# A gated linear attention and MLP kernel: the PSUM bank or shared buffer of every tile named in a table

## The chip, the core and the metric

The kernel runs on one core of one Trainium2 chip, as one program: TensorE multiplies matrices into PSUM, VectorE (DVE), ScalarE (ACT) and GpSimd (POOL) do elementwise work, SyncE (SP) issues nearly all DMAs. Each engine takes its instructions in the order written, and semaphores order the engines against each other. The metric is the device time of one execution in microseconds.

## The reference

Gated linear attention with a recurrent state, then a feed-forward block with a layer norm ahead of it and a residual around it. Shapes: 4 batches, 8 heads, 768 steps, 48 columns a head, so rows of 384; the hidden width is 1536. q, k, v, alpha and g_ln are float32; w_ch1 and w_ch2 come as float64.

```python
for t in range(S):
    state = alpha[:, :, t, :, None] * state + einsum('bhd,bhe->bhde', k[:, :, t], v[:, :, t])
    y[:, :, t] = einsum('bhd,bhde->bhe', q[:, :, t], state)
x = y.transpose(0, 2, 1, 3).reshape(B, S, H * D)
xn = (x - mean(x)) / sqrt(var(x) + 1e-06) * g_ln
out = x + maximum(xn @ w_ch1, 0.0) @ w_ch2
```

## The kernel before

The 768 steps are cut into 6 chunks of 128. The unit of attention is one chunk of one batch, 24 in all, written as generators (`attention`, turns a to x in the order below). For a unit, ScalarE takes the log of alpha (L343), TensorE sums it along the chunk with a triangular matrix (L348, L355) and ScalarE exponentiates the sum (L358, L359); DVE scales q and k by it (L363, L365). q and k are turned round, by TensorE (L422) for the first 12 units and by DVE and DMAs (L404, L150, L416) after that. TensorE makes scores (L435, L450), DVE copies them under a mask out of PSUM into `at` (L464), TensorE makes the state's update (L479) and the output (L515). The state is gated on DVE and POOL (L492, L494). ScalarE reads the output (L524, L525), stores it away in DRAM (L539) and normalises it (L547 to L557), and the row is turned round into `xT` (L573, or L563 and L150).

The feed-forward block of chunk 0 is a plain matrix product: `hidden` (L598, relu in L601) and `project` (L610, L614). For chunks 1 to 5 both products use a scheme of fewer block products with sums ahead of and behind them: DVE adds blocks of xT, of w1, of the hidden values and of w2 (`combine_x` L870, `combine_first` L845, `combine_hidden` L704, `combine_weights` L675); `hidden_product` (L901) and `product` (L722) multiply the blocks, and what they leave in PSUM is copied by ScalarE (L913, L746) or added by DVE and POOL (L917 to L930, L736 to L742). The weights come as float64 and are rounded to float32 in eight pieces by DVE and ScalarE (L247 to L261) in the first 100 us.

The order of all this is written out by hand. `ORDER` (L28) is a string in which each letter advances one generator by one step, and `tc.manual_schedule()` keeps that order on every engine. Waits are worked out by the tile framework from the tiles that an instruction reads and writes.

Tiles come from pools. A tag has `bufs` buffers, and the tiles of a tag share them: `bank` is six PSUM banks, `row` eight buffers of 384 columns, `sum` twelve buffers of 512 columns (the turned q and k, the sums of blocks and the copies `u`), `in` six input buffers, `gate` four, `few` five, `mid` three. Which of its buffers a tile gets is the framework's choice. The first instruction that writes a tile waits until all that used the tile before it in the same buffer has ended, whatever that other tile held. PSUM has two more banks, `updates`, that no tag shares.

In the code before, `combine_hidden` makes its six or seven sum tiles together at its first step (L688), `combine_x` its five (L856), `product` and `hidden_product` their three `u` tiles at the first product of a group (L716, L888), and `attention` its gate tile where the row of gates is sent off (L375).

Of the kernel before, what the change touches and what calls it, by code (L numbers as in the profile page):

```python
# [50 lines left out]

WHERE = {
}


def pick(marks, usual=0):
# [4 lines left out]
def kernel(  # L61
# [36 lines left out]
    nc = tc.nc  # L98
# [11 lines left out]
    assert out.shape == (B, S, DM) and B * P <= 512 and DM + 2 * NP <= 512  # L110

    cpool = ctx.enter_context(tc.tile_pool(name="const", bufs=1))
    raw = ctx.enter_context(tc.tile_pool(name="raw", bufs=B // 2))
    stage = ctx.enter_context(tc.tile_pool(name="stage", bufs=STAGED))
    work = ctx.enter_context(tc.tile_pool(name="work", bufs=2))
    dram = ctx.enter_context(
        tc.tile_pool(name="dram", bufs=B, space=bass.MemoryType.DRAM))
    ps = ctx.enter_context(tc.tile_pool(name="ps", bufs=2, space=bass.MemoryType.PSUM))

    nc.scalar.preload_act_table_set("natural_log_exp_and_others")  # L120

# [205 lines left out]
    def attention(c, b):  # L327
# [44 lines left out]
        ends = slice(P - 1, P) if whole else slice(HS - 1, P, HS)  # L372
        ne = 1 if whole else 2
        row = dram.tile([2, 2 * 64 * NP], FP32, name="row", tag="row")
        gate = work.tile([P, 2, NP], FP32, name="gate", tag="gate", bufs=B)  # L375
        nc.sync.dma_start(row[:ne], eq_of(c, b)[ends].rearrange("o p i c -> o (p i c)"))
        yield
        def load_next():
# [84 lines left out]
        else:  # L463
# [2 lines left out]
                data=scores.pop((c, b)).rearrange("k p s t -> k (p s) t"),  # L466
                mask=mask_of_halves.unsqueeze(1).broadcast_to([P, 2 * NP, HS]))
        yield
        with nc.allow_non_contiguous_dma(reason="two rows to columns"):
            nc.sync.dma_start(gate[:, :ne], row[:ne].rearrange("o (p r) -> r o p", p=NP))  # L470
        yield
# [182 lines left out]
    def summer(name, op):  # L654
        return getattr((nc.vector, nc.gpsimd)[pick(sides[name])], op)
# [57 lines left out]

    def product(c, n):
        if n == SECOND[0]:
            u = [work.tile([P, 512], FP32, name="u", tag="sum", bufs=12) for i in range(3)]  # L716
            win["u"] = [u[i // 2][:, i % 2 * HM:][:, :HM] for i in range(5)]
        acc = held.pop(("S", c, FOLLOWS[n])) if n in FOLLOWS else ps.tile(
            [P, HM], FP32, name="ops", tag="bank", bufs=6)
        lhs, rhs = blocks_of(c)[1][n], weights_ready()[n]  # L720
        for j in range(NT):
            nc.tensor.matmul(acc, lhs[:, j], rhs[:, j], start=j == 0 and n not in FOLLOWS,  # L722
                             stop=j == NT - 1 and n not in FOLLOWS.values(),
                             skip_group_check=True)
        if n in FOLLOWS.values():
            held["S", c, n] = acc
        yield
        e, f, g, q4, r8 = win["u"]
# [15 lines left out]
        copied = {0: e, 2: f, 9: f, 14: g, 13: q4, 8: r8}  # L744
        if n in copied:
            copy(out=copied[n], in_=acc)  # L746
        if n in (15, 3):
            add(o(0))
        elif n == 11:
            sub(o(0))  # L750
        elif n == 18:
            sub(o(1))
            sub(o(3))
        elif n == 10:
            add(o(2))
        elif n == 1:
            sub(o(7))
        elif n in (4, 17):
            add(o(4))
        elif n == 6:  # L760
            sub(o(1))
        elif n == 2:
            late(o(1), e)
            late(o(1), f, "sub")
            send(c, 0)
        elif n == 5:
            nc.vector.tensor_sub(g, acc, g)
        elif n == 19:
            sub(o(3))
            send(c, 1)  # L770
        elif n == 9:
            late(f, g, "sub")
            late(o(2), f, "sub")
            late(o(3), f, "sub")
        elif n == 12:
            sub(o(5))
            add(o(7))
        elif n == 13:
            late(o(5), q4)
            late(o(5), g, "sub")  # L780
            late(r8, q4, "sub")
            late(o(7), r8)
            late(o(6), r8)
            if c + 1 == NCB:
                send(c, 2, slice(0, HM))
                send(c, 3, slice(HM, DM))
        elif n == 7:
            add(o(5))
            if c + 1 == NCB:
                send(c, 2, slice(HM, DM))  # L790
            else:
                send(c, 2)
                send(c, 3, slice(HM, DM))
        elif n == 16:
            add(o(6))
            send(c, 3, slice(0, HM))
        yield
# [51 lines left out]

    def combine_x(c):  # L850
        b = x_blocks(c)
        new = []
        if c + 1 == NCB:
            buffers_of_last()
            new = late_of["x"]
        for i in range(0 if new else 5):  # L856
            t = work.tile([P, NT, P], FP32, name=f"sum{i}", tag="sum", bufs=12)
            t = t.rearrange("p a t -> p (a t)")
            new += [t[:, k * HB * P:(k + 1) * HB * P] for k in range(2)]
        t101, t103, t100, m7, t102, m10, m9, m13, m8 = new[:9]  # L860
        add, sub = "tensor_add", "tensor_sub"
        ready = x_ready(c)
        for n, op, out, x, y in (
                (None, sub, t101, b[1], b[3]), (2, sub, t100, b[4], b[5]),
                (1, add, t103, b[2], t100), (7, add, m7, t101, t103),
                (14, sub, t102, b[0], t100), (10, sub, m10, t102, t101),
                (3, sub, t101, t101, b[5]), (9, sub, m9, b[4], b[0]),
                (5, add, b[4], b[2], b[4]), (13, sub, m13, b[3], t103),
                (8, sub, m8, b[1], t102)):
            summer("X", op)(out, x, y)  # L870
            if n is not None:
                ready[n] = out
            yield
# [8 lines left out]
    def hidden_product(c, r, n):  # L882
# [2 lines left out]
            if c + 1 < NCB:  # L885
                hT_of[c] = work.tile([P, NJ, B, P], FP32, name="hT", tag="hT", bufs=1)
        if n == FIRST[0]:
            for i in range(3):  # L888
                u = late_of["u"][i] if c + 1 == NCB else work.tile(
                    [P, 512], FP32, name="u", tag="sum", bufs=12)  # L890
                first_of["u", c, i] = u.rearrange("p (j t) -> p j t", j=2)
# [11 lines left out]
        if n in JOINS.values():  # L903
            held["F", c, n] = acc
        yield
        u0, u1, u2 = (first_of["u", c, i] for i in range(3))
# [4 lines left out]
        copied = {3: c5, 7: c4, 5: c2, 1: u0, 10: u1, 9: u2, 8: u2, 11: c1, 2: c0}  # L911
        if n in copied:
            nc.scalar.copy(out=copied[n], in_=acc)  # L913
        if n == 5:
            add_late(c2, c2, u1)
        elif n == 6:
            add(c4, acc, c4)  # L917
            add_late(c4, c4, u2)
        elif n == 4:
            sub(c2, c2, acc)  # L920
        elif n == 14:
            add(c0, acc, c0)  # L922
        elif n == 1:
            add_late(c0, c0, u0)
        elif n == 13:
            add(c1, acc, c1)
            add_late(c1, c1, u2)
            add_late(c5, c5, u2)
        elif n == 12:
            sub(c5, c5, acc)  # L930
        elif n == 0:
            nc.scalar.activation(out=c3, in_=acc, func=AFT.Relu)
# [70 lines left out]
```

## Time and profile before

| | |
|---|---|
| Median of 3 runs | 422.12 us (419.4 to 424.57) |
| Profiled execution | 420.36 us |
| Its span, from the first to the last instruction | 418.6 us |
| Granted TensorE clock | 1.000 |
| DMA traffic | 61.25 MB, mean 146 GB/s |

In the profile, PE is TensorE's matmuls, PEld its weight loads (they overlap), SPq SyncE's queue of DMA issues. A line such as L464 is the line of the kernel that issued an instruction, with out<-in by the names of the tiles. A float32 matmul leaves about two records. In a timeline row come the start and the length in us, then engine, line, operation, tiles and shapes; xN merges N like instructions in a row, and a bracket gives the idle time of the engine before it and what ended that. In a list of waits come the total, the number and the longest; in a list of groups busy time and the mean in ns; in a table of windows the length of the stretch and then the busy time of PE, PEld, DVE, ACT and POOL, each with a count, the granted clock, the DMA share and GB/s.

### The profile page before, as it was taken

Reading aid. Unit: us, or ns where it says so; the run is one execution under the profiler, and the core shown is the slowest. Engines: PE = TensorE matmul, PEld = TensorE weight load, DVE = VectorE, ACT = ScalarE, POOL = GpSimd, SP = SyncE. Lnnn points to the kernel's source line nnn. Section 1 sums busy time; section 2 is a strip of 40 time slices with the busy share of each in tenths; the row PEclk is TensorE's granted clock in tenths of the full one; section 3 lists DMA queues with packets and bytes.
Section 4 is the critical chain, followed back from the end, with each engine's and each line's share of the span. In section 5 each row is a group of like instructions: output and inputs, shape, how many; then the busy total and the mean of one; then the engine's idle time right before and its main releaser. Section 6 shows DMA issues by size and latency. Waiting matters only on the chain.

```text
span 418.6 us, 11431 instructions
## 1 busy us (share of the span) xinstructions
PE 409.0 (98%) x4617; PEld 354.6 (85%) x4617; DVE 292.6 (70%) x555; ACT 214.0 (51%) x521; POOL 123.8 (30%) x134
## 2 busy tenths in 40 slices
PE   7999899999999999999989999999999999999997
PEld 5888788866568889998869997889998899999996
DVE  4896988999899749877357954578664195705755
ACT  5788656955255754147672126862265743432310
POOL 1021030120006561243270442371144331617200
PEclk9999999999999999999999999999999999999999
DMA  7987978788578476848762479746223600011201
GB/s 268 311 256 228 290 212 278 209 239 188 182 152 206 102 158 134 231 126 164 208 145 56 72 203 255 141 99 112 62 100 80 156 2 2 0 38 40 75 20 56
DMA packets 134050, 61.25 MB, mean 146 GB/s; under 512 B 90559, under 2 KB 130882, under 8 KB 133998
## 3 DMA queue, kind: packets, MB, share of 16 engines
q1 hardware_dynamic: 133848, 60.37, 55.6%
q8 instruction: 36, 0.59, 0.6%
q10 hardware_dynamic: 150, 0.17, 0.1%
q14 instruction: 16, 0.13, 0.1%
HBM read 43.12 MB, written 17.39 MB: 145 GB/s over the span
## 4 chain that ended last, share of the span: by engine, by line
PE 88%; DMA 4%; DVE 4%; issue 1%; POOL 1%; ACT 1%; SPq 1%; DVEq 0%; POOLq 0%
PE hps L901 31%; PE ops L722 31%; PE ops L610 7%; PE hps L598 5%; PE yps L515 4%; PE ups L479 2%; PE aps L450 2%; DMA ws<-in_moe_w_ch_dram 2%; DMA rq<-in_q_dram 1%; PE lps L355 1%; PE tps L422 1%; DMA vx<-in_v_dram 1%; DVE w L249 1%; PE aps L435 1%; DVE w L247 1%
## 5 line engine op out<-in xcount | busy, mean ns | idle before, releaser
L901 PE MATMUL hps<-sum,w 128*128 128x256 f32 x192 | 46.8, 385 | 0.0
L746 ACT COPY u<-ops 128x192 f32<-128x192 f32 x30 | 9.6, 319 | 64.5 <-PE ops L722 57.3
L494 POOL TENSOR_TENSOR mid<-mid,gate 112x192 f32<-112x192 f32 x20 | 14.0, 703 | 91.5 <-DVE mid L492 71.7
L901 PEld LDWEIGHTS hps<-sum,w 128*128 128x128 f32 x192 | 35.4, 190 | 6.6 <-ACT u L913 1.6
L722 PE MATMUL ops<-w,hT 128*128 128x192 f32 x224 | 40.7, 327 | 0.0
L722 PEld LDWEIGHTS ops<-w,hT 128*128 128x128 f32 x224 | 37.2, 190 | 0.5
L598 PE MATMUL hps<-xT,w 128*128 128x256 f32 x144 | 33.6, 384 | 1.5 <-DVE at L464 1.5
L901 PE MATMUL hps<-xT,w 128*128 128x256 f32 x136 | 33.5, 381 | 0.0
L610 PE MATMUL ops<-w,hT 128*128 128x384 f32 x96 | 32.6, 488 | 0.0
L598 PEld LDWEIGHTS hps<-xT,w 128*128 128x128 f32 x144 | 26.4, 190 | 6.4 <-DVE at L464 1.9
L742 POOL TENSOR_TENSOR ob<-ob,u 128x192 f32<-128x192 f32 x32 | 20.6, 654 | 28.5 <-ACT u L746 14.5
L722 PE MATMUL ops<-ws,sum 128*128 128x192 f32 x160 | 28.9, 327 | 0.0
L901 PEld LDWEIGHTS hps<-xT,w 128*128 128x128 f32 x136 | 25.6, 190 | 3.3
L913 ACT COPY u<-hps 128x512 f32<-128x512 f32 x32 | 18.7, 583 | 18.9 <-PE hps L901 14.6
L913 ACT COPY hT<-hps 128x512 f32<-128x512 f32 x40 | 23.1, 584 | 9.2 <-PE hps L901 7.9
L610 PEld LDWEIGHTS ops<-w,hT 128*128 128x128 f32 x96 | 17.8, 190 | 11.1 <-issue 0.6
L722 PEld LDWEIGHTS ops<-ws,sum 128*128 128x128 f32 x160 | 26.5, 190 | 0.2
L494 POOL TENSOR_TENSOR st<-st,gate 112x192 f32<-112x192 f32 x16 | 16.3, 1017 | 34.3 <-DVE st L492 34.3
L736 DVE TENSOR_TENSOR ob<-ops,ob 128x192 f32<-128x192 f32 x40 | 13.7, 353 | 17.5 <-PE ops L722 11.6
L940 ACT ACTIVATE hT<-hT 128x512 f32<-128x512 f32 x40 | 23.7, 627 | 3.0 <-DVE hT L920 2.4
L722 PE MATMUL ops<-ws,hT 128*128 128x192 f32 x128 | 23.6, 328 | 1.2 <-DVE at L464 1.2
L922 DVE TENSOR_TENSOR hT<-hps,hT 128x512 f32<-128x512 f32 x8 | 5.5, 692 | 26.1 <-ACT hT L913 18.3
(225 smaller groups left out, 1051.8 us busy)
## 6 DMA issues: line engine op xcount, KB each, us to landing
ws<-in_moe_w_ch_dram SPq DMA_DIRECT2D x8, 1152.0 KB
vn<-in_v_dram SPq DMA_DIRECT2D x12, 384.0 KB
kept<-x SPq DMA_DIRECT2D x24, 192.0 KB
ob<-kept SPq DMA_DIRECT2D x24, 192.0 KB
rows<-rj SPq DMA_DIRECT2D x48, 96.0 KB
out_dram<-ob SPq DMA_DIRECT2D x18, 192.0 KB
xrows<-xt SPq DMA_DIRECT2D x64, 48.0 KB
xT<-xrows SPq DMA_DIRECT2D x16, 192.0 KB
```

The source lines that it names most:

```text
L450: nc.tensor.matmul(pair[o][halves[i if o else 1 - i], p, s], k_of[rs, p, s], q_of[rs, p, s], start=True, stop=True)
L494: nc.gpsimd.tensor_mul(new, new, by)
L515: nc.tensor.matmul(yps[j][halves[s], i, p], of, by, skip_group_check=True, start=not (cross and k), stop=k == 1 or not cross)
L598: nc.tensor.matmul(hps, w1[:, f, j * P:(j + 1) * P], xT_of[0][:, f, bs], start=(f == 0), stop=(f == NF - 1))
L610: nc.tensor.matmul(ops_of[b], hT_of[c][:, j, b], w2[:, j], start=(j == 0), stop=(j == NJ - 1))
L722: nc.tensor.matmul(acc, lhs[:, j], rhs[:, j], start=j == 0 and n not in FOLLOWS, stop=j == NT - 1 and n not in FOLLOWS.values(), skip_grou ...
L736: nc.vector.tensor_add(x, acc, x)
L742: getattr(nc.vector if c + 1 == NCB else nc.gpsimd, f"tensor_{op}")(x, x, y)
L746: copy(out=copied[n], in_=acc)
L901: nc.tensor.matmul(acc[:, i], w, b, start=n not in JOINS and i == 0, stop=n not in JOINS.values(), skip_group_check=True)
L913: nc.scalar.copy(out=copied[n], in_=acc)
L940: nc.scalar.activation(out=x, in_=x, func=AFT.Relu)
```

## The change

A table `HOMES` names, for each of seven tags, the buffer of every tile in the order in which the tiles are made: 277 characters for `bank`, 88 for `row`, 138 for `sum`, 27 for `in`, 24 each for `gate` and `few`, 20 for `mid`. A class `Shelf` stands between the kernel and three of its pools; it takes the next character of the tag's string and asks the pool for a tile of a tag of its own with one buffer (`bank_0` to `bank_5` for the banks). The number and size of the buffers stay as they were. Sum tiles, `u` tiles and the gate tile are now made where they are first written, through small functions `new` and `u`, so that the order of the table is the order of writing. No operation is changed.

In the two programs as built, the tile that comes before it in the same buffer is another one for 49 of the 277 bank tiles, 17 of 88 rows, 34 of 138 sum tiles and 2 of 27 input tiles; for gate, few and mid it is the same for all.

```diff
+HOMES = {
+    "in": (
+        "012345012304512350412350142",
+    ),
+    "bank": (
+        "01234501243015243014235014253014230252501245340243241024153043032150342121031230",
...
+    ),
+    "row": (
+        "01234567012345763217604325607761352743740365214724753607541605321756035042371562",
+        "04317204",
+    ),
+    "sum": (
+        "10325476a8b940216375b9081a35426987b06a29a176954a3b8701a2695a904b219b6085234a80b1",
...
+}
+
+class Shelf:
+    def __init__(self, pool):
+        self.pool = pool
+        self.homes = {tag: "".join(homes) for tag, homes in HOMES.items()}
+
+    def tile(self, shape, dtype, **how):
+        homes = self.homes.get(how.get("tag"))
+        if homes is not None:
+            tag = how["tag"]
+            how |= {"tag": f"{tag}_{homes[0]}", "bufs": 1}
+            self.homes[tag] = homes[1:]
+        return self.pool.tile(shape, dtype, **how)
...
-    raw = ctx.enter_context(tc.tile_pool(name="raw", bufs=B // 2))
+    raw = Shelf(ctx.enter_context(tc.tile_pool(name="raw", bufs=B // 2)))
-    work = ctx.enter_context(tc.tile_pool(name="work", bufs=2))
+    work = Shelf(ctx.enter_context(tc.tile_pool(name="work", bufs=2)))
-    ps = ctx.enter_context(tc.tile_pool(name="ps", bufs=2, space=bass.MemoryType.PSUM))
+    ps = Shelf(ctx.enter_context(
+        tc.tile_pool(name="ps", bufs=2, space=bass.MemoryType.PSUM)))
...
-        gate = work.tile([P, 2, NP], FP32, name="gate", tag="gate", bufs=B)
         nc.sync.dma_start(row[:ne], eq_of(c, b)[ends].rearrange("o p i c -> o (p i c)"))
...
+        gate = work.tile([P, 2, NP], FP32, name="gate", tag="gate", bufs=B)
         with nc.allow_non_contiguous_dma(reason="two rows to columns"):
             nc.sync.dma_start(gate[:, :ne], row[:ne].rearrange("o (p r) -> r o p", p=NP))
...
     def combine_hidden(c):
         a, ready = blocks_of(c)
-        n0, n2, n6, n9, n5, n13, *more_of = (
-            work.tile([P, NT, P], FP32, name=f"sum{i}", tag="sum", bufs=12)
-            for i in range(6 + (c + 1 == NCB)))
-        n14 = (more_of or [n13])[0]
+        tiles = {}
+
+        def new(i):
+            if i not in tiles:
+                tiles[i] = work.tile([P, NT, P], FP32, name=f"sum{i}", tag="sum", bufs=12)
+            return tiles[i]
+
+        n0, n2, n6, n9, n5, n13 = range(6)
+        n14 = 6 if c + 1 == NCB else n13
...
+            o, x, y = (new(t) if isinstance(t, int) else t for t in (o, x, y))
...
     def product(c, n):
         if n == SECOND[0]:
-            u = [work.tile([P, 512], FP32, name="u", tag="sum", bufs=12) for i in range(3)]
-            win["u"] = [u[i // 2][:, i % 2 * HM:][:, :HM] for i in range(5)]
+            win["u"] = {}
...
+        def u(i):
+            if i // 2 not in win["u"]:
+                win["u"][i // 2] = work.tile([P, 512], FP32, name="u", tag="sum", bufs=12)
+            return win["u"][i // 2][:, i % 2 * HM:][:, :HM]
```

`combine_x` and `hidden_product` are changed in the same way, and the uses of the tiles with them.

More of the change, by code (lines that the diff above doesn't have):

```diff
@@ L53 @@
 }
+HOMES = {
[4 more added lines that the diff above has]
+        "01234501243015243014235014253014230252501245340243241024153043032150342121031230",
+        "41350241305214325320151204122213421423151531543152045345324105240132534520142130",
+        "51304531253102432514132510245132054205025015345342051205105314253142035410241032",
+        "5032451034020251243240240530421534012",
+    ),
[5 more added lines that the diff above has]
+        "10325476a8b940216375b9081a35426987b06a29a176954a3b8701a2695a904b219b6085234a80b1",
+        "75462370a54973a94b17856a234109ba786324597380b216a5407382b9",
+    ),
+    "gate": (
+        "012301230123012301230123",
+    ),
+    "few": (
+        "012340123042132041302413",
+    ),
+    "mid": (
+        "01201201201201201201",
+    ),
+}
[10 more added lines that the diff above has]
+        return self.pool.tile(shape, dtype, **how)
 def pick(marks, usual=0):
@@ L727, in product @@
         yield
-        e, f, g, q4, r8 = win["u"]
+        def u(i):
+            if i // 2 not in win["u"]:
+                win["u"][i // 2] = work.tile([P, 512], FP32, name="u", tag="sum", bufs=12)
+            return win["u"][i // 2][:, i % 2 * HM:][:, :HM]
         def o(k):
@@ L742, in late @@
             getattr(nc.vector if c + 1 == NCB else nc.gpsimd, f"tensor_{op}")(x, x, y)
-        copied = {0: e, 2: f, 9: f, 14: g, 13: q4, 8: r8}
+        copied = {0: 0, 2: 1, 9: 1, 14: 2, 13: 3, 8: 4}
         if n in copied:
-            copy(out=copied[n], in_=acc)
+            copy(out=u(copied[n]), in_=acc)
         if n in (15, 3):
@@ L762, in product @@
         elif n == 2:
-            late(o(1), e)
-            late(o(1), f, "sub")
+            late(o(1), u(0))
+            late(o(1), u(1), "sub")
             send(c, 0)
         elif n == 5:
-            nc.vector.tensor_sub(g, acc, g)
+            nc.vector.tensor_sub(u(2), acc, u(2))
         elif n == 19:
@@ L771, in product @@
         elif n == 9:
-            late(f, g, "sub")
-            late(o(2), f, "sub")
-            late(o(3), f, "sub")
+            late(u(1), u(2), "sub")
+            late(o(2), u(1), "sub")
+            late(o(3), u(1), "sub")
         elif n == 12:
@@ L778, in product @@
         elif n == 13:
[L779 to L783, printed above, removed]
+            late(o(5), u(3))
+            late(o(5), u(2), "sub")
+            late(u(4), u(3), "sub")
+            late(o(7), u(4))
+            late(o(6), u(4))
             if c + 1 == NCB:
@@ L851, in combine_x, with new @@
         b = x_blocks(c)
-        new = []
+        tiles = {}
         if c + 1 == NCB:
             buffers_of_last()
[L855 to L860, printed above, removed]
+        def new(i):
+            if c + 1 == NCB:
+                return late_of["x"][i]
+            if i // 2 not in tiles:
+                t = work.tile([P, NT, P], FP32, name=f"sum{i // 2}", tag="sum", bufs=12)
+                tiles[i // 2] = t.rearrange("p a t -> p (a t)")
+            return tiles[i // 2][:, i % 2 * HB * P:][:, :HB * P]
+        t101, t103, t100, m7, t102, m10, m9, m13, m8 = range(9)
         add, sub = "tensor_add", "tensor_sub"
@@ L869, in combine_x @@
                 (8, sub, m8, b[1], t102)):
+            out, x, y = (new(t) if isinstance(t, int) else t for t in (out, x, y))
             summer("X", op)(out, x, y)
@@ L887, in hidden_product @@
         if n == FIRST[0]:
[L888 to L891, printed above, removed]
+            first_of["u"] = {}
         cs = [third_of(c, t, h)[:, 2 * r:2 * r + 2].rearrange("p j b t -> p j (b t)")
@@ L905, in hidden_product, with u @@
         yield
-        u0, u1, u2 = (first_of["u", c, i] for i in range(3))
+        def u(i):
+            if i not in first_of["u"]:
+                t = late_of["u"][i] if c + 1 == NCB else work.tile(
+                    [P, 512], FP32, name="u", tag="sum", bufs=12)
+                first_of["u"][i] = t.rearrange("p (j t) -> p j t", j=2)
+            return first_of["u"][i]
         c0, c1, c2, c3, c4, c5 = cs
@@ L909, in hidden_product @@
         add_late = nc.gpsimd.tensor_add
-        copied = {3: c5, 7: c4, 5: c2, 1: u0, 10: u1, 9: u2, 8: u2, 11: c1, 2: c0}
-        if n in copied:
-            nc.scalar.copy(out=copied[n], in_=acc)
+        copied = {3: c5, 7: c4, 5: c2, 11: c1, 2: c0}
+        spare = {1: 0, 10: 1, 9: 2, 8: 2}
+        if n in copied or n in spare:
+            nc.scalar.copy(out=u(spare[n]) if n in spare else copied[n], in_=acc)
         if n == 5:
-            add_late(c2, c2, u1)
+            add_late(c2, c2, u(1))
         elif n == 6:
             add(c4, acc, c4)
-            add_late(c4, c4, u2)
+            add_late(c4, c4, u(2))
         elif n == 4:
@@ L923, in hidden_product @@
         elif n == 1:
-            add_late(c0, c0, u0)
+            add_late(c0, c0, u(0))
         elif n == 13:
             add(c1, acc, c1)
-            add_late(c1, c1, u2)
-            add_late(c5, c5, u2)
+            add_late(c1, c1, u(2))
+            add_late(c5, c5, u(2))
         elif n == 12:
```

## The prediction

> **What bounds the kernel now.** I read the page's engine totals first, then the list of TensorE's waits, then the same list for its weight loads, then the chain of waits.
>
> ```profile
> span 418.6 us, 11431 instructions
> PE 409.0 (98%) x4617; PEld 354.6 (85%) x4617; DVE 292.6 (70%) x555; ACT 214.0 (51%) x521; POOL 123.8 (30%) x134
> PE 88%; DMA 4%; DVE 4%; issue 1%; POOL 1%; ACT 1%; SPq 1%; DVEq 0%; POOLq 0%
> ```
>
> TensorE is busy for 409.0 of 418.6 us and carries 88% of the chain that ends last. So a wait that disappears is worth something only where it stops TensorE, and all of TensorE's visible idle time is 418.6 - 409.0 = 9.6 us. Its waits over 150 ns are these (in total, times, longest, all in us), first for matmuls, then the rows that matter here for weight loads:
>
> ```profile
> PE tps L422 <- DVE qk L363: 1.8, 1, 1.8
> PE hps L598 <- DVE at L464: 1.5, 1, 1.5
> PE ops L722 <- DVE at L464: 1.2, 1, 1.2
> PE lps L283 <- DVE more L280: 1.1, 1, 1.1
> PE yps L515 <- issue: 1.0, 1, 1.0
> ...
> PEld hps L901 <- ACT u L913: 1.6, 7, 0.3
> PEld ops L722 <- DVE at L464: 1.5, 1, 1.5
> ...
> PEld lps L355 <- ACT x L524: 0.5, 1, 0.5
> ```
>
> Two of them look wrong for the mathematics. The hidden product (L598) reads xT and w1, the output product (L722) reads weights and hidden values; neither reads the score tile that DVE's masked copy (L464) takes out of PSUM. They wait because the new accumulator was given the bank that the score tile had. The same holds for L355, which has nothing to do with the ScalarE copy of yps in L524. These three are the kind of wait that the table can change; L422, L283 and the issue stall are not.
>
> Is a busy TensorE a full one? Two stretches of the chain tell:
>
> ```profile
> 310.83 26.63 PE hps L901 x120
> ...
> 389.36 26.17 PE ops L722 x160
> ```
>
> 26.63 / 120 = 0.222 us for records of 256 columns, 26.17 / 160 = 0.164 us for 192 columns: a ratio of 1.357 for a ratio of columns of 1.333, so the spacing follows the columns and no wait sits in it. [...]
>
> **The change, part by part.** In the two built programs each engine has the same instructions in the same order (PE 2371, DVE 547, ACT 477, SP 434, POOL 139). No operation is added, none is moved past another, and no transfer is issued in another place of its queue. What differs is the buffer of a tile, hence whose readers its first writer waits for: 114 instructions wait for something else (PE 54, ACT 29, DVE 20, SP 9, POOL 2). Making the sum tiles and the gate tile later changes no instruction by itself; the gate, few and mid tiles follow the same tile in their buffer as before, so these cost nothing.
>
> First stall. TensorE's hidden tiles from 48.04 us on, the relu that frees the new bank, and the copy it waits for today:
>
> ```profile
> 48.04 2.96 PE L598 MATMUL hps<-xT,w 128*128 128x256 f32 x12
> 52.49 3.72 PE L598 MATMUL hps<-xT,w 128*128 128x256 f32 x16 [1.50 <-DVE at L464]
> ...
> 51.72 0.72 DVE L464 COPY_PREDICATED at<-consts,aps 128x512 f32<-128x512 int32 x1
> ...
> 49.73 0.39 ACT L601 ACTIVATE hT<-hps 128x256 f32<-128x256 f32 x1 [1.70 <-PE hps L598]
> ```
>
> The new order puts this accumulator behind the hidden tile whose relu ends at 49.73 + 0.39 = 50.12, before TensorE is free at 52.49 - 1.50 = 50.99. Gain 1.50 us. The masked copy's bank now goes to the group after next, 12 records of 0.222 us later, at 50.99 + 2.66 = 53.65; the copy ends at 51.72 + 0.72 = 52.44, 1.2 us before that.
>
> Second. The lower half of the decay sum (L355) waits for the read of a yps bank:
>
> ```profile
> 112.58 0.56 DVE L614 TENSOR_TENSOR ob<-ops,ob 128x384 f32<-128x384 f32 x1 [0.95 <-PE ops L610]
> ...
> 113.67 0.33 ACT L524 ACTIVATE x<-yps 128x192 f32<-128x192 f32 x1 [6.22 <-PE yps L515]
> ...
> 114.14 0.19 PEld L355 LDWEIGHTS lps<-la,consts 64*64 64x64 f32 x4 [0.54 <-ACT x L524]
> ```
>
> In the new order its bank was last read by the L614 that ends at 113.14, ahead of the weight load's free time of 113.60. Gain 0.54 us at most; the matmul row does not show the stall, because the modelled ends of the first half's matmuls cover it. I take 0.5.
>
> Third, again L464 ahead of a product that needs none of it:
>
> ```profile
> 216.55 1.46 PE L722 MATMUL ops<-w,hT 128*128 128x192 f32 x8
> 219.19 1.57 PE L722 MATMUL ops<-ws,hT 128*128 128x192 f32 x8 [1.17 <-DVE at L464]
> ...
> 216.84 0.58 ACT L932 ACTIVATE hT<-hps 128x512 f32<-128x512 f32 x1
> ```
>
> The new predecessor is read by L932, done at 217.42, before 219.19 - 1.17 = 218.02. Gain 1.17; the next product, which takes over the copied bank, would start 8 records of 0.164 us later, at 219.33, and the copy is done when it releases the row at 219.19.
>
> What is late next? Between the first and the second place DVE is nearly full and feeds TensorE the rounded weights:
>
> ```profile
> 50.00:85.00 35.00, 33.50 (x554) 27.26 (x552) 31.71 (x49) 24.69 (x61) 6.57 (x8) 1.00 0.81 240
> 85.00:115.00 30.00, 29.01 (x345) 18.27 (x344) 27.42 (x45) 12.95 (x38) 2.84 (x5) 1.00 0.74 198
> ...
> 81.79 1.55 DVE L261 SCALAR_TENSOR_TENSOR w<-w,ws 128x1152 f32<-128x1152 f32 x1
> ...
> 82.44 2.75 PE L610 MATMUL ops<-w,hT 128*128 128x384 f32 x8
> ...
> 102.63 0.71 ACT L557 ACTIVATE xn<-x,few 128x384 f32<-128x384 f32 x1
> ...
> 104.31 0.49 PE L573 MATMUL xps<-consts,xn 128*128 128x128 f32 x3
> ...
> 61.85 1.35 ACT L253 ACTIVATE ws<-ws,small 128x1152 int32<-128x1152 int32 x1
> ...
> 63.23 1.36 DVE L255 SCALAR_TENSOR_TENSOR ws<-ws 128x1152 int32<-128x1152 int32 x1 [1.19 <-ACT ws L253]
> ```
>
> (The third busy time of a window is DVE's: 31.71 of 35 and 27.42 of 30 us.) The piece rounded last (81.79 + 1.55 = 83.34) is first used by the fourth output matmul of the row at 82.44, six of its eight records later, by 82.44 + 6 x 2.75 / 8 = 84.50: a margin of 1.2 at most. The transpose at 104.31 has 104.31 - 103.34 = 0.97 after the normalised row. If DVE keeps its times, only about 1.0 of the first 1.50 gets through. But DVE itself idled 1.19 for ScalarE's L253, which stood behind a relu that TensorE now feeds earlier; if that moves, so does DVE, and 1.5 gets through. I take 1.2, between the two.
>
> New waits. The tightest are hidden tiles that now follow each other's relus, and none ends a wait at the times of this trace:
>
> ```profile
> 58.74 7.97 PE hps L598 x36
> ...
> 60.27 0.38 ACT L601 ACTIVATE hT<-hps 128x256 f32<-128x256 f32 x1 [0.71 <-PE hps L598]
> ```
>
> The third group of six records starts at 58.74 + 12 x 7.97 / 36 = 61.40, the relu that it now waits for ends at 60.65: 0.75 to spare, and both move together, since the relu follows TensorE. ACT and DVE also take on waits for landings in their queues. The closest in time is the log of alpha (L343, the second of the row), which now waits for the row of x that was sent off 8 us before:
>
> ```profile
> 23.34 0.48 SPq L539 DMA_DIRECT2D kept<-x  x1
> ...
> 31.32 0.95 ACT L343 ACTIVATE la<-ra 128x384 f32<-128x384 f32 x2
> ```
>
> Were one late, the PSUM reads queued behind it on ACT would hold a bank and so TensorE. I put them at 0; the far end is 1 us of loss, about the largest stall in TensorE's list short of the 1.8.
>
> Other addresses. All shared SBUF buffers move. Matmuls that read a shared sum buffer and matmuls that read xT, which lies elsewhere, cost nearly the same now:
>
> ```profile
> L901 PE MATMUL hps<-sum,w 128*128 128x256 f32 x192 | 46.8, 385 | 0.0
> ...
> L901 PE MATMUL hps<-xT,w 128*128 128x256 f32 x136 | 33.5, 381 | 0.0
> ```
>
> 4 ns by 192 records is 0.8 us either way; I take 0.
>
> Sum: 1.2 + 0.5 + 1.17 = 2.9 us, between a loss of 1 + 0.8 = 1.8 and a gain of 3.2 + 0.8 = 4.0. Against the profiled execution of 420.36 us (span 418.6) that is 417.5, a span of 415.7. That execution lies 1.8 us below the median of the three runs, 422.12, which themselves spread over 5.2 us; against the median it is 419.2 us.
>
> **Rivals.** (a) The gain is taken back by DVE between 50 and 115 us: TensorE arrives earlier and waits for rounded weights instead. Only the third place and a part stay, 1.2 us: 420.9. For it the 90% of DVE, against it the 1.19 us that DVE waits for ScalarE.
>
> (b) Slower. ScalarE's L253 keeps its place in the queue while TensorE runs ahead, so relus pile up behind it, and banks that now pass from relu to relu come free late. The row at 61.85 is one of three between 50 and 75 us, 1.35 us each. It decides where a relu comes more than 0.75 us late for the next group. All three felt in full would cost 3 x 1.35 = 4.05 against a gain of 2.9: 422.12 + 1.2 = 423.3. Against it: the relu rows there wait for TensorE, not for ScalarE.
>
> (c) More than the visible idle time comes back, because busy matmuls hide waits as at 113.6 us. The seven waits of L901's weight loads on ScalarE, 1.6 us, would be such, and the 1.5 of the first place in full: 419.2 - 1.9 = 417.3. Against it stands the spacing of the matmuls. [...]
>
> (d) The table changes nothing that is felt: the three banks come out as I read, but the scheduler's waits at the same place are replaced by others just as late. 422.1. Against it the release times worked out above.
>
> **Chances.** Forecast 0.56, (a) 0.18, (b) 0.12, (c) 0.07, (d) 0.07. The range adds the scatter of the runs, about 2.5 us around the median, to cases from (c) to (b): 415.8 to 423.6. 2%, 8.4 us, is about what a measurement of this kernel can tell from no change. Faster by more than that would need nearly all of the 9.6 us that TensorE idles: 0.04. Slower by more would need about six of the eight L253 (8.4 / 1.35) felt in full and no gain, or something that I do not see: 0.06. Within: 0.90.
>
> **What would show it.** In the changed kernel's list of TensorE waits both rows on L464 should be gone and PEld's L355 on L524 too; PE's idle total should fall from 9.6 to about 7; the span should be near 415.7 with the stretch from 115 us on ending as much earlier as it began. If (a) holds, a new wait of TensorE on L258, L261, L492 or L557 between 50 and 105 us appears; if (b), waits of L598 on L601. A row of TensorE waiting for a landing of qT or kT, or L901 means that differ from 385 and 381 ns, would prove the parts on landings and addresses wrong.

## The result, and the profile after

| | before | after |
|---|---|---|
| Median, us (runs) | 421.46 (20) | 417.91 (20) |
| Lowest to highest, us | 418.28 to 424.57 | 415.64 to 422.35 |
| Profiled execution, us | 420.36 | 416.19 |
| Its span, us | 418.6 | 414.4 |

The ratio is 0.9921, with a 95% interval of 0.9899 to 0.9943: 421.46 x 0.0079 = 3.3 us faster (the two medians lie 3.55 apart). The two profiled executions differ by 4.2.

In the code after, L464 has become L510, L598 L645, L601 L648, L610 L657, L363 L410, L355 L402, L722 L774, L515 L562, L901 L958, L253 L300 and L255 L302. First the engine totals and the chain that ended last, from the page of the changed kernel:

```profile
span 414.4 us, 11430 instructions
...
PE 407.1 (98%) x4617; PEld 353.9 (85%) x4617; DVE 293.0 (71%) x555; ACT 213.4 (51%) x521; POOL 126.2 (30%) x134
...
PE 97%; DMA 1%; SPq 0%; issue 0%; DVE 0%; DVEq 0%
```

TensorE is idle for 414.4 - 407.1 = 7.3 us instead of 9.6, and the chain hardly leaves it any more. Its whole list of matmul waits (in total, times, longest):

```profile
PE tps L468 <- DVE qk L410: 3.0, 1, 3.0
PE lps L330 <- DVE more L327: 1.1, 1, 1.1
PE yps L562 <- issue: 0.2, 1, 0.2
```

Both rows that named the masked copy are gone. Among the weight loads, the wait of the decay sum on the yps copy is gone too, and 0.2 us of the 1.5 on the masked copy is left (L774 on L510). The first row has grown by 1.2 us, but that stands at the start, and TensorE starts the tps tile behind it at 9.19 us against 9.05 before: the matmuls ahead of it were over earlier. Busy time of the engines in three stretches (PE, PEld, DVE, ACT, POOL, then clock, DMA share, GB/s), to be held against the same stretches of before:

```profile
50.00:85.00 35.00, 35.00 (x651) 28.95 (x649) 33.43 (x52) 25.13 (x61) 8.19 (x9) 1.00 0.85 254
85.00:115.00 30.00, 29.85 (x284) 18.39 (x279) 28.13 (x47) 15.46 (x46) 2.46 (x4) 1.00 0.76 202
115.00:219.00 104.00, 104.00 (x1316) 90.54 (x1308) 76.58 (x146) 57.22 (x133) 45.10 (x42) 1.00 0.71 163
```

From 50 to 85 us TensorE was busy for 33.50 us and is now busy for all 35.00: the 1.50 of the first place. From 85 to 115 it gained 0.84, which is the issue stall at L515 (0.99 before, 0.15 after), and from 115 to 219 the 0.98 of the third place's 1.17 that falls in that stretch. The second place does not show in busy time. It shows in the length of the decay sum's group of matmuls, here before and after (start, length, both in us):

```profile
113.44 1.56 PE L355 MATMUL lps<-la,consts 64*64 64x384 f32 x8
```

```profile
111.13 0.84 PE L402 MATMUL lps<-la,consts 64*64 64x384 f32 x8
```

The same eight records took 1.56 us and take 0.84: 0.72 us of waiting had been booked as busy time. Among the waits of the weight loads, the 0.5 us of L402 on L571 stand in e1 and e4, which have the second place as before, and not in e2, e3 and e9 to e12, which have it as in the change. So 1.50 + 0.72 + 1.17 = 3.4 us came back at the three places, and 0.84 more in these two executions from the issue stall. That the first place needs other tiles of the table for its 1.50 is what the experiments show.

### The profile page after: what moved, and what is told of

Same layout as the page of the kernel before. It is cut to its first block, busy times and chain, and to the rows that moved or that the text cites. A ratio compares the mean times of both kernels' runs of the same rounds, so it can differ in the third digit from the quotient of the medians.

```text
span 414.4 us, 11430 instructions
## 1 busy us (share of the span) xinstructions
PE 407.1 (98%) x4617; PEld 353.9 (85%) x4617; DVE 293.0 (71%) x555; ACT 213.4 (51%) x521; POOL 126.2 (30%) x134
## 4 chain that ended last, share of the span: by engine, by line
PE 97%; DMA 1%; SPq 0%; issue 0%; DVE 0%; DVEq 0%
PE hps L958 32%; PE ops L774 32%; PE hps L645 8%; PE ops L657 8%; PE yps L562 5%; PE tps L468 3%; PE aps L496 3%; PE ups L526 3%; PE lps L402 2%; DMA rq<-in_q_dram 1%; PE aps L481 1%; PE yps L552 1%; PE xps L620 1%; PE lps L395 0%; SPq L213 0%
## 5 line engine op out<-in xcount | busy, mean ns | idle before, releaser
L958 PE MATMUL hps<-sum,w 128*128 128x256 f32 x192 | 46.8, 385 | 0.0
L958 PEld LDWEIGHTS hps<-sum,w 128*128 128x128 f32 x192 | 35.4, 190 | 6.6 <-ACT u L977 1.6
L774 PE MATMUL ops<-w,hT 128*128 128x192 f32 x224 | 40.8, 327 | 0.0
L774 PEld LDWEIGHTS ops<-w,hT 128*128 128x128 f32 x224 | 37.1, 190 | 0.7 <-DVE at L510 0.2
L958 PE MATMUL hps<-xT,w 128*128 128x256 f32 x136 | 33.5, 381 | 0.0
L645 PE MATMUL hps<-xT,w 128*128 128x256 f32 x144 | 33.2, 382 | 0.0
L657 PE MATMUL ops<-w,hT 128*128 128x384 f32 x96 | 32.6, 488 | 0.0
L645 PEld LDWEIGHTS hps<-xT,w 128*128 128x128 f32 x144 | 26.4, 190 | 4.5 <-PE aps L496 0.6
L774 PE MATMUL ops<-ws,sum 128*128 128x192 f32 x160 | 28.9, 327 | 0.0
L958 PEld LDWEIGHTS hps<-xT,w 128*128 128x128 f32 x136 | 25.6, 190 | 3.3
L541 POOL TENSOR_TENSOR st<-st,gate 112x192 f32<-112x192 f32 x16 | 18.2, 1140 | 32.6 <-DVE st L539 32.6
L657 PEld LDWEIGHTS ops<-w,hT 128*128 128x128 f32 x96 | 17.8, 190 | 11.1 <-issue 0.6
L774 PEld LDWEIGHTS ops<-ws,sum 128*128 128x128 f32 x160 | 26.5, 190 | 0.2
L774 PE MATMUL ops<-ws,hT 128*128 128x192 f32 x128 | 23.5, 327 | 0.0
```

What stands on the lines that cost most here:

```text
L541: nc.gpsimd.tensor_mul(new, new, by)
L645: nc.tensor.matmul(hps, w1[:, f, j * P:(j + 1) * P], xT_of[0][:, f, bs], start=(f == 0), stop=(f == NF - 1))
L657: nc.tensor.matmul(ops_of[b], hT_of[c][:, j, b], w2[:, j], start=(j == 0), stop=(j == NJ - 1))
L958: nc.tensor.matmul(acc[:, i], w, b, start=n not in JOINS and i == 0, stop=n not in JOINS.values(), skip_group_check=True)
```

## The experiments

All are tables: an experiment changes which tile precedes which in a buffer, and nothing else; every engine has the same instructions in the same order in all of them. Names of banks are arbitrary, so strings look more different than they are. What the names of the experiments stand for, for bank tiles (times of before; in brackets what ends the earlier tile's use, in the lines of after):

```
place          tile, starts at     earlier tile before        earlier tile in the change
first          hps 52.49           aps (DVE L510)             hps (ACT L648)
               and hps, hps, lps behind it, which take over the banks exchanged
next           hps 61.37           lps (DVE L410)             hps (ACT L648)
               hps 62.66           aps (DVE L510)             hps (ACT L648)
               hps 63.96           hps (ACT L648)             lps (DVE L410)
               hps 65.25           hps (ACT L648)             aps (DVE L510)
second         lps 114.14          yps (ACT L571)             ops (DVE L661)
               and two aps
third          ops 219.19          aps (DVE L510)             hps (ACT L996)
               and the ops behind it
```

The ratios of all twelve runs, each to the kernel before on the same chip:

| | ratio | 95% interval |
|---|---|---|
| e1 old table | 1.000 | 0.9976 to 1.0025 |
| e2 banks as in the change, rest old | 0.9917 | 0.9884 to 0.9950 |
| e7 banks old, rest as in the change | 0.998 | 0.9955 to 1.0005 |
| e4 first place alone | 0.9988 | 0.9961 to 1.0016 |
| e8 first place and the swap at 61.37 us | 0.9958 | 0.9927 to 0.9988 |
| e3 first, second and third place | 0.9975 | 0.9947 to 1.0002 |
| e5 the three places and the next | 0.9879 | 0.9836 to 0.9921 |
| e10 the same again | 0.9905 | 0.9863 to 0.9946 |
| e6 the change without the three places (banks) | 1.0019 | 0.9986 to 1.0051 |
| e9 the change | 0.9877 | 0.9836 to 0.9917 |
| e11 the change without the next | 0.9966 | 0.9937 to 0.9996 |
| e12 the change without the third | 0.9957 | 0.9922 to 0.9991 |

**Is it the table's order, and which rows of it?** In e1 every tile follows the tile that it followed in the kernel before:

```diff
     "in": (
-        "012345012304512350412350142",
+        "013245012304512350412350142",
...
     "bank": (
-        "01234501243015243014235014253014230252501245340243241024153043032150342121031230",
+        "50124350142503142504213504231504215232352304150351325032514024054130524105415021",
...
```

> The new code with a table that names, for every tile, the buffer which the kernel before had given it: every wait is again that of the kernel before, while the table, the tiles made late and the new code stay. Theory (the gain is TensorE's three stalls on banks, nothing else): ratio 1.000 to the kernel before, stalls of 1.5 us at the hidden product and 1.2 us at the output product are back. Rival (addresses, code or the time at which tiles are made carry part of it): ratio 0.992 to 0.997 and the stalls are back all the same. The unforecast stall of about 1 us at the state product near 91 us: back if it belongs to the place of the work, gone if it belongs to the code.

Measured 1.000, and the stalls are back in TensorE's list:

```profile
PE yps L562 <- issue: 1.7, 2, 1.1
PE hps L645 <- DVE at L510: 1.4, 1, 1.4
PE tps L468 <- DVE qk L410: 1.3, 1, 1.3
PE ops L774 <- DVE at L510: 1.2, 1, 1.2
```

So the new code and tiles made late are worth nothing by themselves. e2 and e7 split the table (diffs against the change; the other rows as in e1 or in the change):

```diff
 e2  "row": (
-        "01234567012345763217604325607761352743740365214724753607541605321756035042371562",
+        "01234567012345736217304625307731652746740365124747153601572650341062536574301624",
...
 e7  "bank": (
-        "01234501243015243014235014253014230252501245340243241024153043032150342121031230",
+        "50124350142503142504213504231504215232352304150351325032514024054130524105415021",
...
```

> The bank row of the table as in the change, the rows of row, sum and in tiles as the kernel before chose: 54 waits of TensorE and 4 of ScalarE are new, those of the SBUF buffers are old. Theory: the whole gain, ratio 0.992 (0.990 to 0.994). Rival (the SBUF buffers carry part by letting VectorE or ScalarE start earlier): 0.994 or higher.

> Banks as in the kernel before, rows of row, sum and in tiles as in the change (25 waits of ScalarE, 20 of VectorE, 9 of SyncE, 2 of GpSimd are new). Theory: nothing, 1.000 (0.998 to 1.002), all three stalls back. Rival (VectorE is earlier near 52 us and the stall shrinks): 0.997.

Measured 0.9917 and 0.998. The banks carry the gain; the 53 SBUF tiles with another predecessor, and all SBUF addresses, are worth no more than their interval, 0.45% of 422 us or 1.9 us at the utmost.

**Are the three places enough?** e4 has the first alone, e3 all three (against e1, then against e4):

```diff
 e4  "bank": (
-        "50124350142503142504213504231504215232352304150351325032514024054130524105415021",
+        "50124350142503142504213504231504215232352304150351325032514024043510423504354025",
...
 e3  "bank": (
...
-        "34120534102543152150242503255521523521343413451342054154125304250312415420352310",
+        "34120534102543152150242503255521352351242412431245034134153204530215413450235210",
...
```

> All choices as in the kernel before but at the first of the three places (four tiles, six waits): the hidden-product bank near 52 us is taken from ScalarE's copy and not from VectorE's. Theory: 1.5 us alone, ratio 0.9964, the stall on VectorE near 52 us gone, that at 219 us still there. Rival (the stall near 91 us goes with the first): 2.3 us, ratio 0.9945, no stall at the state product near 90 us. Rival of the prediction (VectorE has only 1.2 us of margin around 84 and 104 us and takes part back): 1.2 us or less, ratio 0.997 or higher, and a new TensorE wait on VectorE between 84 and 105 us.

> All choices as in the kernel before but at three places in the bank row (nine tiles, 13 waits): the hidden-product tiles around 52 us, the three tiles from the second lps of 114 us on, and two output-product tiles at 219 us. Theory: all of the gain, 1.5 + 0.5 + 1.2 = 3.2 us, ratio 0.992. Rival (the other 40 banks, whose waits TensorE does not show as stalls, matter through many small idles): a third or more of the gain is missing, ratio 0.994 to 0.996.

Both missed. With the first place alone the ratio is 0.9988, and TensorE's list and timeline say why:

```profile
PE hps L645 <- DVE qk L410: 1.6, 1, 1.6
```

```profile
57.23 2.96 PE L645 MATMUL hps<-xT,w 128*128 128x256 f32 x12
...
61.78 3.07 PE L645 MATMUL hps<-xT,w 128*128 128x256 f32 x13 [1.59 <-DVE qk L410]
...
60.24 0.76 DVE L298 TENSOR_SCALAR ws<-ws 128x1152 int32<-128x1152 int32 x1
60.92 0.35 DVE L539 TENSOR_TENSOR mid<-ups,st 112x192 f32<-112x192 f32 x1
61.18 0.54 DVE L410 TENSOR_TENSOR qk<-rk,lps 128x384 f32<-128x384 f32 x1
```

The stall at 52 us was gone and stood again 9 us later, on the hidden tile whose bank a decay sum had held. VectorE reads that decay sum in L410, and its rows leave no gap ahead of it: VectorE, not the bank, was late. In the kernel before, the same wait ended without harm, since TensorE came 1.5 us later and found the read done (VectorE's row there, against 61.37 for the tile):

```profile
60.16 0.55 DVE L363 TENSOR_TENSOR qk<-rk,lps 128x384 f32<-128x384 f32 x1
```

60.16 + 0.55 = 60.71 leaves 0.66 us, less than half of what the first place had gained. 1.50 - 0.66 would be a stall of 0.84; it was 1.59 here and 1.19 in e3, because VectorE's own times differ from one execution to the next (its read in e4 began 1.0 us later, at 61.18). The theory was changed to: the first term needs the next swaps too. e8 adds one of them to e4, e5 both to e3:

```diff
 e8  "bank": (
-        "50124350142503142504213504231504215232352304150351325032514024043510423504354025",
+        "50124350142503142504213504231504215232352304150351325032514024043510423534054325",
...
 e5  "bank": (
-        "50124350142503142504213504231504215232352304150351325032514024043510423504354025",
+        "50124350142503142504213504231504215232352304150351325032514024043510423535045324",
...
```

> The first place and the one swap behind it, on whose bank TensorE stood for 1.6 us at 62 us in the run with the first place alone; all else as in the kernel before. Theory: the first term of the sum comes through, 1.2 to 1.5 us, ratio 0.9968, the stall at 219 us stands. Rival (the stall walks on to the bank 1.3 us behind, at 63 us, or to 68 us): 0.9985, with a stall on VectorE there.

> The three places and two more swaps of hidden-product banks right behind the first (four tiles near 61 to 64 us, which in the kernel before take banks that VectorE's transposes and masks release, and in the change banks that TensorE or ScalarE released earlier). Theory as changed by the run with three places (there the stall of 1.5 us taken away at 52 us stood again as 1.2 us at 62 us, on the next bank that waits for VectorE): with the next two swapped as well the gain comes through, ratio 0.993, no hidden-product stall on VectorE before 85 us. Rival 1 (VectorE is simply late in this stage and the stall walks on to 68 to 73 us, where tps and yps banks wait for it): 0.9965, a stall on VectorE between 66 and 75 us. Rival 2 (the stalls with no releaser at the state product near 72 and 91 us, 1 to 1.8 us in the runs with old banks and 0.2 to 0.3 us with new ones, are what the other banks buy): 0.995, and these stalls are still over 1 us together.

In e8, measured 0.9958, the time alone decides little: it lies 0.0030 below e4, and each of the two intervals reaches 0.003 to either side. The trace decides. TensorE runs through what e4 had cut in two, and is busy all the time from 50 to 85 us:

```profile
56.92 7.89 PE L645 MATMUL hps<-xT,w 128*128 128x256 f32 x35
...
50.00:85.00 35.00, 35.00 (x651) 28.79 (x650) 33.13 (x53) 24.90 (x61) 7.15 (x9) 1.00 0.84 247
```

e5 has 13 bank tiles of the change's 49 and no other, and its ratio, 0.9879, is no worse than the change's and clear of e3's 0.9975. No wait of TensorE on VectorE stands in its list behind 20 us, so the first rival fell. The second fell with 0.7 us of stalls without a releaser instead of over 1, and with the ratio. For the converse, e6 leaves the three places out of the change's banks, the SBUF rows being old:

```diff
     "bank": (
-        "01234501243015243014235014253014230252501245340243241024153043032150342121031230",
+        "50124350142503142504123504132504125131350143245142140514032542502315042323503205",
...
```

> The bank row as in the change but at the three places, which stand as in the kernel before (40 tiles new, 9 old; the stall at 52 us and that at 219 us are back). Theory: no gain by itself, since TensorE arrives 1.5 us late at everything behind 52 us: ratio 0.998 to 1.000. Rival (the other banks carry a gain of their own, by stalls that the profile has no releaser for): 0.996 or less.

Measured 1.0019: 40 new banks without the three, the next swaps among them, are worth nothing. Last, four on one chip: the change itself, e5 again, and the change without the next swaps and without the third place:

```diff
 e11 "bank": (
-        "01234501243015243014235014253014230252501245340243241024153043032150342121031230",
+        "50124350142503142504123504132504125131350143245142140514032542521035241052102501",
...
 e12 "bank": (
...
-        "51304531253102432514132510245132054205025015345342051205105314253142035410241032",
+        "30254320132051241302041305123041532153513503423421530153053402134021543205120541",
...
```

> The changed kernel itself, on the chip of the three runs beside it. Both theories: ratio 0.992 (0.990 to 0.994) to the kernel before, no TensorE stall on a bank from 50 us on; the idle with no releaser at the state product near 89 us is anywhere from 0.1 to 1.9 us, if it belongs to the execution and not to the banks (so it stood in the nine runs profiled until now, with old and with new banks).

> The five places (13 tiles) once more, beside the changed kernel. Theory: the five places are all that the change does to the time, so it equals the changed kernel, 0.992 (within 0.002 of it). Rival (the first run's 0.988 is a true gain over the change, because the other 36 banks and the 53 SBUF tiles cost something): 0.988, and 1.5 us below the changed kernel.

> The change, but for the two swaps right behind the first place (four hidden-product tiles at 61 to 64 us, four waits of TensorE), which stand as in the kernel before. Theory (they carry the first term through): the stall on VectorE's qk near 61 us is there, 1.2 to 1.6 us, and the ratio is 0.995 to 0.996. Rival (the rest of the table covers it, the run with the first place alone having lost it elsewhere): 0.992 and no such stall.

> The change, but for the two output-product tiles at 219 us, which stand as in the kernel before. Theory: the stall on VectorE's transpose is back there with 1.17 us, the ratio is 0.9949, and everything up to 214 us is as in the change. Rival (TensorE, now earlier by 3 us, meets VectorE later still): 0.997 or above, a stall of 2 us or more.

Measured 0.9877, 0.9905, 0.9966 and 0.9957. e9 is the changed kernel and lies 0.0044 below its first measurement (0.9921), so a distance of that size between two versions says little. By that measure the five places (0.9879 and 0.9905) do what the change does, and no version here beats it. Without the next swaps more than half of the gain is lost, and the wait on L410 is back, though with less than expected. How much the next swaps are worth is not fixed: against e9 the loss is 3.7 us, against the first measurement 1.9, and with the intervals anything from 0.3 to 6; the profile of e11 shows the 0.7 of the wait and an issue stall of 1.0 near 72 us. Without the third place its stall is back (TensorE's lists of e11 and e12):

```profile
PE hps L645 <- DVE qk L410: 0.7, 1, 0.7
```

```profile
PE ops L774 <- DVE at L510: 1.1, 1, 1.1
```

## Why the prediction was right, and where it was not

**The bound, and which waits go.** Right. The three waits were read from TensorE's lists as waits for a bank's last tenant, and all three went; e1 and e6 have all three back and the time of before, and e5 gets the whole gain with five places. L422 (now L468), L283 (now L330) and the issue stall were said to be out of the table's reach. The first two are; of the stall the last section tells more.

**First term, 1.2 us: measured 1.50 in the change, mis-sized.** It was cut to 1.2 because VectorE's margins of 1.2 at 84.5 us and 0.97 at 104 us would bind if VectorE kept its times. It did not keep them. Timeline of the change, the rows that answer to the margin at 84.5 and to the idle 1.19 us behind L253 (now L300):

```profile
80.33 1.54 DVE L308 SCALAR_TENSOR_TENSOR w<-w,ws 128x1152 f32<-128x1152 f32 x1
...
80.94 2.75 PE L657 MATMUL ops<-w,hT 128*128 128x384 f32 x8
...
61.48 0.56 DVE L412 TENSOR_TENSOR qk<-rq,eq 128x384 f32<-128x384 f32 x1
61.94 1.36 DVE L302 SCALAR_TENSOR_TENSOR ws<-ws 128x1152 int32<-128x1152 int32 x1
...
60.07 0.38 ACT L648 ACTIVATE hT<-hps 128x256 f32<-128x256 f32 x1 [0.91 <-PE hps L645]
60.35 1.38 ACT L300 ACTIVATE ws<-ws,small 128x1152 int32<-128x1152 int32 x1
```

The relu that TensorE feeds comes earlier, L300 behind it starts at 60.35 instead of 61.85, and L302 starts without a gap, 1.29 us earlier than its 63.23 of before. The last rounding ends at 81.87 instead of 83.34, 1.47 us earlier, and the matmul that needs it starts at 80.94 + 6 x 2.75 / 8 = 83.00: the margin is 1.1 as it was. VectorE had been late because TensorE was. This is the second of the two cases that the prediction set out and took the middle of.

**The step that failed: what carries the first term.** The prediction put the bank tiles outside the three places, 40 of them, at nothing, and looked at their new waits only as a risk. Four of them, the two next swaps, are the cover of the first term. The tile that it weighed with "0.75 to spare" behind its new relu, at 61.40, is the very tile whose old wait, on VectorE's read of the decay sum, had only 0.66 us to spare: it listed what is late next at 84.5 and 104 us, but did not move TensorE forward against the old waits in between. Taken alone, the first place measured 0.0012 x 421.43 = 0.5 us; the interval (a loss of 0.7 to a gain of 1.6) does not exclude 1.2, but the trace of e4 shows its stall standing again at 61.78. That the forecast came out all the same is luck in this part: the change happens to hold these swaps as well.

**Second term, 0.5: 0.72** by the length of the group, above the 0.54 that the weight load's row gave as the most; **third, 1.17: 1.17** by its row, and e12 without it lies 0.008 above e9, with intervals too wide to size it. **New waits and addresses, 0: right.** No stall on a bank or a landing stands in TensorE's list after 50 us, and L958's two groups have the means of before:

```profile
L958 PE MATMUL hps<-sum,w 128*128 128x256 f32 x192 | 46.8, 385 | 0.0
...
L958 PE MATMUL hps<-xT,w 128*128 128x256 f32 x136 | 33.5, 381 | 0.0
```

**The sum.** 2.9 us forecast, 3.3 measured. Of the 1.3 us between 419.2 and 417.91, 0.7 is the base (422.12 from three runs, 421.46 from twenty), 0.4 the size of the terms, and 0.2 the step from the ratio's 3.3 to the 3.55 between the medians. The span of 414.4 against 415.7 is 0.4 of the terms and 0.84 of the issue stall, which the prediction did not count; it stands between 0 and 2.3 in all profiles, and at 0.2 and 2.3 in two of the changed kernel. The 8.4 us that the prediction called about the least to be told from no change was too much: over twenty executions the interval is 0.9 us to either side.

**Rivals.** (a) fell: VectorE took nothing back, being 95% busy from 50 to 85 us (33.43 of 35). What (a) describes did happen in e4 and e3, with another wait than those it named. (b) fell: no wait of L645 on L648 appears. (c), at 417.3, was nearer in time than the forecast and right in part: the first place gave its 1.5 in full, and the 0.72 us was a wait inside busy time. The 1.6 us of waits of L901's weight loads that it counted on did not go; L958's stand at 1.6 again. (d) fell.

## What to carry to other kernels

The tile framework lets a buffer's next tile wait for the last reader of the tile before it, so a wait on something that the mathematics does not need is a wait on a neighbour in the table. Giving the buffer to a tile whose reader is earlier removed it here: the 1.50 and 1.17 us that TensorE waited for L464 are gone from its list. Before pricing one such wait, move everything behind it forward by its size and look through the waits of the kernel before for margins smaller than that: here the next one was 0.66 us, 9 us later. With the first place alone the stall came back there with 1.6 us, and only with that tile's bank swapped as well did it go. An engine that looks like the next limit may be late only because it is fed late; its own idle rows, and what ended them, tell that (here 1.19 us of VectorE's behind ScalarE's L253: in the change this idle time is gone, and the rounding behind it starts 1.29 us earlier).

## What the runs showed of the hardware

**The issue stall.** In the middle of a run of short state products (L562, or L515 before) TensorE stops where its list names no releaser. The page of the profile lists a queue of the kind instruction, q8, with 36 packets and 0.59 MB. In the traces of the kernel before and of the change, one of these packets starts a little ahead of the stall (all in us):

```
             packet starts   idle at L562   TensorE goes on   after the packet's start
before       88.92           0.99           91.30             2.38
the change   86.64           0.15           88.95             2.31
```

The two distances lie within 0.1 us of each other, while the stalls differ by 0.84. That the packet has to do with the stall is not shown: it is one of 36, and no run changed them. The stall's size is not the table's alone: the changed kernel has 0.15 us in its first profile and 2.29 in e9. It is 0.53 us in e6 and 1.94 in e8, and the lists of e7 and e12 have none.

A second such stall of 0.7 to 1.1 us near 72 us stood in e1, e3, e4 and e11, all with the old banks of the next swaps, and in none of the eight profiles with the new ones (e8 has one of the two swaps), where TensorE is busy from 50 to 85 us but for e6's 1.3 us on L510; the other two with the old ones had none either. So this stall may be part of what the next swaps take away. No run takes it apart from the wait on VectorE, and this stays open.

**The clock at the start.** In five of the fourteen profiles (e2, e3, e7, e10, e12) the granted clock falls near 10 us, about where TensorE's wait for the first tps tile (L468) ends, and its mean over the first 50 us is 0.97; in the others it is 1.00. Windows of e2, then the same ten microseconds of the change:

```profile
10.00:12.00 2.00, 2.00 (x9) 1.26 (x8) 0.88 (x2) 0.59 (x1) 0.00 (x0) 0.54 0.93 279
12.00:14.00 2.00, 2.00 (x14) 1.65 (x14) 1.13 (x3) 1.15 (x3) 0.00 (x0) 0.61 0.95 278
14.00:16.00 2.00, 2.00 (x31) 1.78 (x30) 1.63 (x4) 1.15 (x3) 0.00 (x0) 1.00 0.99 315
```

```profile
10.00:20.00 10.00, 10.00 (x169) 7.90 (x169) 8.80 (x18) 7.53 (x18) 0.00 (x0) 1.00 1.00 293
```

2 x 0.46 + 2 x 0.39 = 1.7 us of full clock are lost, about half of what the change gains, and the same kernel has it or not: e5 and e10 have the same table, and only e10 shows it. The loss is as large in the other four, by the clocks of their first two stretches of ten microseconds: 0.98 and 0.85 in e3, 0.97 and 0.86 in e7, 0.95 and 0.88 in e10, 0.99 and 0.84 in e12, each time 10 x 0.17 = 1.7 us. The lowest that a stretch of 2 us shows is 0.50 (e7, from 10 to 12 us).

The length of the wait alone does not decide it. TensorE waits 1.7 to 2.1 us for the tile in the five profiles with the loss (e7 the least, e3 the most). Without the loss it waits 1.3 to 3.0 us, among them 1.8 in the kernel before. No run changed this wait, and what lowers the clock is not shown.

The ratios carry some of this. The profiled executions with the loss show a mean clock of 0.995 or 0.996, the other nine 0.999 or 1.000. Executions at 0.996 or less are 3 of 6 in e9 and 9 of 12 in e12, so part of the distance between these two may be the clock and not the third place.
